# A segment loop reordered: the last keys summed in two banks, the second scores, sums and exponential moved forward

## The chip, the core and the metric

The kernel runs on one core of one Trainium2 chip. The metric is the device time of one execution in microseconds (us), as the median of several runs. TensorE multiplies matrices (PE in the profile, its weight loads PEld), VectorE and ScalarE work element by element (DVE, ACT), GpSimd does the same without access to the accumulation banks (POOL), and SyncE issues transfers (SP). All engines run at once, each through its own list of instructions in order, and wait for one another by semaphores.

## What is computed

```python
def _A_ref(x, mem0, Wq, Wk, Wv, Wo, seg_len):          # B=1, S=2048, Dm=512, H=32, Dh=128, M=8, seg_len=32
    ...
    mem = mem0
    for s in range(n_seg):                              # 64 segments
        xs = x[:, s * seg_len:(s + 1) * seg_len, :].copy()
        h = jnp.concatenate([mem, xs], axis=1)          # 8 memory rows and 32 rows of x
        q, k, v = (jnp.einsum('btd,dhe->bhte', h, W) for W in (Wq, Wk, Wv))
        scores = jnp.einsum('bhqe,bhke->bhqk', q, k) * scale
        scores = jnp.where(mask[None, None], scores, -1000000000.0)
        p = _softmax(scores, axis=-1)
        o = jnp.einsum('bhqk,bhke->bhqe', p, v)
        o = jnp.einsum('bhte,hed->btd', o, Wo)
        mem = o[:, :M, :].copy()
        outs.append(o[:, M:, :])
    return jnp.concatenate(outs, axis=1)
...
h = x + _A_ref(_layernorm(x, axis=-1), A_mem0, A_Wq, A_Wk, A_Wv, A_Wo, A_seg_len)
h2 = h + _B_ref(_layernorm(h, axis=-1), B_w_in, B_w_sp, B_b_sp, B_w_out)
```

(The three projections stand on one line here.) Block A is recurrent: the first eight rows of a segment's output are the memory rows of the next, so the 64 segments run one after another. Block B, a gated layer over the whole sequence, follows; the change doesn't touch it.

## The kernel before

Every operation is recorded through a small planner that keeps, for each engine, its instructions in the order in which the program names them, and derives the semaphore waits from tokens: a tile is read or written, and an accumulation bank is one token ("ps", bank). So the order of the calls in the loop is the order in which each engine works, and nothing is rearranged afterwards. PE's own instructions wait for PE's only through that order.

There are eight accumulation banks of 128 x 512 numbers. In the loop, a segment's inner 32 rows (8 of memory and the first 24 of x) are the stationary operand: a 128 x 32 weight, and four such products run side by side in the four column strips of the array (c = 0 to 3). Below, four matmuls that run side by side count as one group. The 512 input features are four chunks (dc), so a sum takes four groups. The 32 heads are two halves b of 16. The last 8 rows of x of each segment don't depend on the memory, and their queries, keys and values are computed ahead for 16 segments at a time.

One segment in PE's order, before the change:

- Queries (mi = 0) and keys (mi = 1) of half 0, in banks 0 and 1, eight groups by `QK`, with `mem_out` in between, which forms the second half of this segment's memory rows from the segment before (`hTm` is its token, copied by ACT at L685). `QK_evac` copies a sum to the tile Tst on ACT (L519), and DVE transposes it in 32 x 32 blocks into QT or KT (L532). `mask_put` writes the mask to the bank, onto which the scores are added.
- Queries of half 1 in bank 6, then keys of half 1 in bank 7, four groups of 512 columns each. The keys leave by two ACT copies of 256 columns and two DVE transposes (`parts` = 2).
- `S_half`, scores of half 0 (L554, L560), in bank 0; `sm_exp`, the exponential on ACT (L568), to E_sb.
- Values: `V_half` of half 0 in bank 6 and half 1 in bank 2; the first chunk of both, then the other three of half 0. `V_evac` copies them on DVE (L615).
- `sm_sums` of half 0: matmuls with ones that sum E_sb (L575, and L496 for the four that keep their weights); on ACT the logarithm `sm_ln` (L586) and `sm_rcp` (L590), an exponential of its negative, give the reciprocal of the sum.
- Scores of half 1, exponential, the last three chunks of the values of half 1, sums, logarithm, reciprocal.
- `sm_norm` multiplies E_sb by the reciprocal, in two instructions (L594 for the inner rows, L598 for the last eight): half 0 on POOL, half 1 on DVE.
- One item of work for later segments, in bank 3 (XB): a group of queries or keys (L414, four heads, 16 matmuls of 128 x 128 tiles), of values (L433), or, from segment 48 on, of block B (L775).
- `PV_half`, probabilities times values (L623, L629), both halves in banks 0, 1, 6 and 7, with the array cut by rows; copies on ACT and DVE (L642, L644); the output product of rows computed ahead (L707); the output product `Wo`, and the first half of the next memory rows.

A matmul marked as held keeps the weights that its strip has already; the others load theirs first. A held matmul has line L496 in the profile, one with a load L495. `lastop` keeps marks (the last instruction of the queries, keys, scores and values) for which transfers into reused memory wait. In segment 0 the loop also computes values ahead (`start_v`), through banks 3, 4 and 5 in turn.

Of the kernel before, what the change touches and what calls it, by code (L numbers as in the profile page):

```python
# [8 lines left out]
U32 = mybir.dt.uint32  # L9
# [160 lines left out]
def fast_path(nc, st, keep, A_x, A_mem0, A_Wq, A_Wk, A_Wv, A_Wo, A_seg_len, B_w_in, B_w_sp, B_b_sp, B_w_out, out):  # L170
# [95 lines left out]
    def PB(b):  # L266
        return ("ps", b)
# [116 lines left out]
    def slot(s):  # L384
        return s % NSLOT
# [93 lines left out]


    QKB = {(0, 0): 0, (0, 1): 1, (1, 0): 6, (1, 1): 7}
    SBK = (0, 1)
    PVB = (0, 1, 6, 7)
    VB = (6, 2)
# [16 lines left out]
    def QK(s, b, mi, dcs, first, last, held=None):  # L501
        ws = (w_q, w_k)[mi]
        bank = QKB[(b, mi)]
        sl = slot(s)
        for dc in dcs:
            for c in range(4):
                rhs = ws[:, dc, :].rearrange("p (h c i) -> p c h i", c=4, i=32)[:, c, 16 * b:16 * b + 16, :]
                pe(lambda e, dc=dc, c=c, rhs=rhs: tile_mm(e, ps[32 * c:32 * c + 32, bank, :], hT[:, sl, dc, :], rhs,
                                                          dc == first, dc == last, c, dc == held),
                   reads=[("hTx", (s // 4) % 3), ("hTm", s, dc // 2), ("W", mi, 2 * b), ("W", mi, 2 * b + 1)], writes=[PB(bank)])  # L510

    def QK_evac(s, b, mi, parts=1):
        bank = QKB[(b, mi)]
        tb = mi
        n = 8 // parts
        for k in range(parts):
            tok = [("T", tb, 0), ("T", tb, 1)] if parts == 1 else [("T", tb, k)]
            cs = slice(64 * n * k, 64 * n * (k + 1))
            act(lambda e, cs=cs: e.activation(out=Tst[:, tb, cs].rearrange("p (hp i r) -> p hp i r", i=32, r=2),  # L519
                                              in_=ps[:, bank, cs].rearrange("p (hp r i) -> p hp i r", r=2, i=32), func=ACT.Copy),  # L520
                reads=[PB(bank)], writes=tok)
        for k in range(parts):
            tok = [("T", tb, 0), ("T", tb, 1)] if parts == 1 else [("T", tb, k)]
            src = Tst[:, tb, 64 * n * k:64 * n * (k + 1)].bitcast(U32)
            hs = slice(n * k, n * (k + 1))
            if mi == 0:
                dst = QT[:, b, hs, :, :].rearrange("p hp q r -> p (hp q r)").bitcast(U32).rearrange("p (hp q) -> p hp q", hp=n)[:, :, 8:40]
                wr = [("QT", b)]
            else:
                dst = KT[:, b, hs, :, :].rearrange("p hp q r -> p (hp q r)").bitcast(U32)  # L530
                wr = [("KT", b, 0), ("KT", b, 1)] if parts == 1 else [("KT", b, k)]
            dve(lambda e, dst=dst, src=src: e.transpose(out=dst, in_=src), reads=tok, writes=wr)  # L532
# [67 lines left out]
    def V_half(s, b, dcs=range(DC), held=None):  # L600
        bank = VB[b]
        sl = slot(s)
        for dc in dcs:
            for c in range(4):
                c0 = (16 * b + 4 * c) * DH
                pe(lambda e, dc=dc, c=c, c0=c0: tile_mm(e, ps[32 * c:32 * c + 32, bank, :], hT[:, sl, dc, :], w_v[:, dc, c0:c0 + 512],
                                                        dc == 0, dc == DC - 1, c, dc == held),
                   reads=[("hTx", (s // 4) % 3), ("hTm", s, dc // 2), ("W", 2, 2 * b), ("W", 2, 2 * b + 1)], writes=[PB(bank)])

    def V_evac(b, eng):  # L610
        bank = VB[b]
        if eng == "act":
            act(lambda e: e.activation(out=V_sb[:, b, :], in_=ps[:, bank, :], func=ACT.Copy), reads=[PB(bank)], writes=[("V", b)])
        else:
            dve(lambda e: e.tensor_copy(out=V_sb[:, b, :], in_=ps[:, bank, :]), reads=[PB(bank)], writes=[("V", b)])  # L615
# [329 lines left out]
    for s in range(NSEG):  # L945
# [12 lines left out]
        if s == 4:  # L958
            load_xe(3, 1)

        QK(s, 0, 0, (0, 1), 0, 3)
        if s > 0:
            mem_out(s - 1, 1)
        QK(s, 0, 1, (1, 0), 1, 2, None if s else 1)
        QK(s, 0, 0, (2, 3), 0, 3)
        QK_evac(s, 0, 0)
        mask_put(0)
        QK(s, 0, 1, (3, 2), 1, 2, 3)
        QK_evac(s, 0, 1)
        mask_put(1)  # L970
        for mi in range(2):
            QK(s, 1, mi, ((2, 0, 1, 3), (3, 0, 1, 2))[mi], (2, 3)[mi], (3, 2)[mi], (2, 3)[mi])
            lastop["qk"[mi]] = em.by_eng["pe"][-1]
            QK_evac(s, 1, mi, 1 + mi)
        if s == 0:
            ebank[:] = [3, 4, 5]
            for n in range(2):
                start_v(n)
        S_half(s, 0)
        sm_exp(0)  # L980
        V_half(s, 0, (0,))
        if s > 0:
            V_half(s, 1, (0,), 0)
        V_half(s, 0, (1, 2, 3))
        V_evac(0, "dve")
        sm_sums(0)
        sm_ln(0)
        S_half(s, 1)
        lastop["s"] = sops[s] = em.by_eng["pe"][-1]
        sm_exp(1)  # L990
        sm_rcp(0)
        if s == 0:
            for n in range(2, 4):
                start_v(n)
        V_half(s, 1, (1, 2, 3) if s > 0 else range(DC))
        lastop["v"] = em.by_eng["pe"][-1]
        sm_sums(1)
        sm_ln(1)
        sm_rcp(1)
        if s == NSEG - 1:  # L1000
# [1107 lines left out]
```

## Time and profile before

| | |
|---|---|
| median of three runs | 855.01 us (853.56 to 855.67) |
| the profiled execution | 853.86 us |
| its span, first to last instruction | 851.7 us |
| mean granted TensorE clock | 1.000 |
| HBM traffic | 42.38 MB read, 21.59 MB written |

The profile is one execution. Its page gives busy time by engine, a chain of work followed back from the end, and groups of instructions by line; further views give the instructions in order of time. Several rows for one line are possible, since a row merges neighbours of one form. Starts and lengths are in us. Ends of matmuls are modelled: a matmul's row lasts longer than the slot after which the next begins, so PE's pace is read from starts.

### The profile page before, as it was taken

What the parts mean: (1) busy time and instruction counts of PE and PEld (TensorE: products, weight loads), DVE (VectorE), ACT (ScalarE), POOL (GpSimd) and SP (SyncE); (2) the same over time, 40 slices, a digit from 0 to 9 for tenths busy, and PEclk for the clock granted to TensorE, in tenths of its full rate; (3) what the DMA queues carried; (4) which work ended last, traced back from release to release, by engine and by line L of the source; (5) the groups of instructions that cost most, each with busy time, mean ns of one, the idle gap of its engine ahead of it and who ended that gap; (6) DMA issues with size and microseconds to landing.
All of it is one profiled execution on the core that took longest, in us unless ns stands there. A gap on an engine that the chain in (4) does not pass through costs nothing.

```text
span 851.7 us, 43893 instructions
## 1 busy us (share of the span) xinstructions
PE 837.0 (98%) x20921; PEld 447.0 (52%) x19133; DVE 538.8 (63%) x1256; ACT 427.1 (50%) x1151; POOL 159.8 (19%) x404
## 2 busy tenths in 40 slices
PE   6999999999999999999999999999999999999997
PEld 5754445555555555556555555555554544444443
DVE  3456677676666666676766666767666676553443
ACT  2455565656555655555655555565656566500000
POOL 5111121122121112121212121211112123200000
PEclk9999999999999999999999999999999999999999
DMA  9972322223212122121323222233322369032001
GB/s 319 379 227 59 75 56 57 54 47 82 57 34 75 34 65 62 26 72 47 64 58 85 55 74 51 81 70 85 91 57 80 96 184 366 2 112 105 33 12 40
DMA packets 105614, 77.21 MB, mean 91 GB/s; under 512 B 63304, under 2 KB 90960, under 8 KB 105424
## 3 DMA queue, kind: packets, MB, share of 16 engines
q1 hardware_dynamic: 105424, 74.35, 30.3%
q8 instruction: 159, 2.61, 1.3%
q14 instruction: 31, 0.25, 0.1%
HBM read 42.38 MB, written 21.59 MB: 75 GB/s over the span
## 4 chain that ended last, share of the span: by engine, by line
PE 95%; DMA 2%; SPq 1%; issue 0%; ACT 0%; DVE 0%; POOL 0%; POOLq 0%
PE f_ps L495 46%; PE f_ps L1183 11%; PE f_ps L496 8%; PE f_ps L414 6%; PE f_ps L707 4%; PE f_ps L1300 3%; PE f_ps L623 3%; PE f_ps L1176 2%; PE f_ps L433 2%; PE f_ps L775 2%; PE f_ps L554 1%; PE f_ps L575 1%; DMA f_arena<-in_A_Wk_dram 1%; PE f_ps L629 1%; PE f_ps L439 1%; PE f_ps L680 1%
## 5 line engine op out<-in xcount | busy, mean ns | idle before, releaser
L495 PE MATMUL f_ps<-f_arena,f_hT 128*32 128x512 bf16 x5120 | 359.5, 380 | 0.3
L495 PEld LDWEIGHTS f_ps<-f_arena,f_hT 128*32 128x32 bf16 x5120 | 117.0, 95 | 153.7 <-issue 63.0
L519 ACT ACTIVATE f_Tst<-f_ps 128x512 bf16<-128x512 f32 (+1 forms) x320 | 150.0, 510 | 77.5 <-PE f_ps L495 77.4
L495 PE MATMUL f_ps<-f_arena,f_cT 128*32 128x256 bf16 x3844 | 127.9, 272 | 0.7 <-ACT f_cT L642 0.5
L495 PEld LDWEIGHTS f_ps<-f_arena,f_cT 128*32 128x32 bf16 x3844 | 94.8, 96 | 27.3 <-ACT f_cT L642 18.2
L615 DVE CAST f_V_sb<-f_ps 128x512 bf16<-128x512 f32 x128 | 88.6, 692 | 25.4 <-PE f_ps L495 25.4
L1183 PE MATMUL f_ps<-f_arena 128*128 128x512 bf16 x448 | 100.9, 379 | 0.6 <-DMA f_arena<-wT_d 0.6
L532 DVE STREAM_TRANSPOSE f_QT<-f_Tst 128x256 uint32<-128x256 uint32 x128 | 57.0, 446 | 68.6 <-ACT f_Tst L519 68.5
L496 PE MATMUL f_ps<-f_arena,f_hT 128*32 128x512 bf16 x1024 | 99.8, 379 | 0.0
L539 POOL COPY f_QT<-f_arena 128x256 bf16<-128x256 bf16 x64 | 30.8, 482 | 313.3 <-PE f_ps L560 313.2
L642 ACT ACTIVATE f_cT<-f_ps 128x320 bf16<-128x320 f32 x128 | 49.0, 435 | 49.1 <-PE f_ps L629 49.1
L644 DVE TENSOR_SCALAR f_cT<-f_ps 128x320 bf16<-128x320 f32 x128 | 56.9, 487 | 25.4 <-PE f_ps L629 25.4
L532 DVE STREAM_TRANSPOSE f_KT<-f_Tst 128x128 uint32<-128x128 uint32 (+1 forms) x192 | 64.5, 349 | 12.9 <-ACT f_Tst L519 12.9
L1183 PEld LDWEIGHTS f_ps<-f_arena 128*128 128x128 bf16 x448 | 43.7, 98 | 53.4 <-DVE f_mv L723 1.0
L673 DVE CAST f_part<-f_ps 128x256 bf16<-128x256 f32 x64 | 27.2, 425 | 67.9 <-PE f_ps L495 67.9
L414 PE MATMUL f_ps<-f_hTe,f_arena 128*128 128x128 bf16 x1024 | 66.9, 223 | 2.2 <-DMA f_arena<-in_A_Wq_dram 1.4
L414 PEld LDWEIGHTS f_ps<-f_hTe,f_arena 128*128 128x128 bf16 x1024 | 59.1, 100 | 7.5 <-ACT f_hTe L395 1.6
L586 ACT ACTIVATE f_R_sb<-f_ps 128x160 f32<-128x160 f32 x128 | 39.1, 305 | 35.9 <-PE f_ps L496 32.7
L1189 DVE TENSOR_TENSOR f_arena<-f_ps,f_arena 128x512 f32<-128x512 f32 x28 | 19.3, 690 | 52.9 <-PE f_ps L1183 52.9
L685 ACT ACTIVATE f_hT<-f_ps 128x16 bf16<-128x16 f32 x126 | 23.3, 185 | 53.4 <-PE f_ps L680 53.0
L671 ACT ACTIVATE f_part<-f_ps 128x256 bf16<-128x256 f32 x64 | 24.6, 385 | 48.4 <-PE f_ps L495 48.4
L544 DVE CAST f_ps<-f_mask 128x224 f32<-128x224 bf16 x128 | 47.1, 368 | 0.0
(118 smaller groups left out, 1094.1 us busy)
## 6 DMA issues: line engine op xcount, KB each, us to landing
wT_d<-f_wst SPq DMA_DIRECT2D x32, 256.0 KB, 2.5
f_arena<-wT_d SPq DMA_DIRECT2D x32, 256.0 KB, 4.8
f_arena<-in_A_Wq_dram SPq DMA_DIRECT2D x4, 1024.0 KB, 8.7
f_arena<-in_A_Wk_dram SPq DMA_DIRECT2D x4, 1024.0 KB, 14.3
f_arena<-in_A_Wv_dram SPq DMA_DIRECT2D x4, 1024.0 KB, 14.5
f_arena<-in_A_Wo_dram SPq DMA_DIRECT2D x8, 512.0 KB, 9.5
f_Vx<-vext_d SPq DMA_DIRECT2D x63, 64.0 KB, 2.9
vext_d<-f_Vs SPq DMA_DIRECT2D x24, 128.0 KB, 2.0
```

The costliest lines, as they stand in the source:

```text
L414: pe(lambda e, h=h, dc=dc, hh=hh: e.matmul(ps[:, bank, hh * 128:(hh + 1) * 128], lhsT=ws[:, dc, h * DH:(h + 1) * DH], rhs=hTe[:, ck % 3, d ...
L495: return e.matmul(out, lhsT=lhsT, rhs=rhs, start=start, stop=stop, skip_group_check=True, tile_position=(0, 32 * c))
L496: return e.add_instruction(mybir.InstMatmult(name=nc.get_next_instruction_name(), ins=[e.lower_ap(rhs), e.lower_ap(lhsT)], outs=[e.lower_a ...
L519: act(lambda e, cs=cs: e.activation(out=Tst[:, tb, cs].rearrange("p (hp i r) -> p hp i r", i=32, r=2), in_=ps[:, bank, cs].rearrange("p (h ...
L532: dve(lambda e, dst=dst, src=src: e.transpose(out=dst, in_=src), reads=tok, writes=wr)
L544: dve(lambda e: e.tensor_copy(out=ps[:, bank, 0:224], in_=mask[:, :]), reads=["mask"], writes=[PB(bank)])
L586: act(lambda e: e.activation(out=R_sb[:, b, :], in_=ps[:, bank, 224:384], func=ACT.Ln, scale=LNS), reads=[PB(bank)], writes=[("R", b)])
L615: dve(lambda e: e.tensor_copy(out=V_sb[:, b, :], in_=ps[:, bank, :]), reads=[PB(bank)], writes=[("V", b)])
L642: act(lambda e: e.activation(out=dst, in_=src, func=ACT.Copy, scale=UNSC), reads=[PB(PVB[c])], writes=[("cT", c)])
L644: dve(lambda e: e.tensor_scalar(out=dst, in0=src, scalar1=UNSC, scalar2=None, op0=ALU.mult), reads=[PB(PVB[c])], writes=[("cT", c)])
L707: pe(lambda e, h=h, g=g, i=8 * qr + bg: e.matmul(ps[32 * g:32 * g + 32, WXB, :], lhsT=cTx[:, rb % 2, i, :], rhs=w_o[:, h, :], start=(i < 4 ...
L1183: pe(lambda e: e.matmul(ps[:, bank, 0:TB], lhsT=z2[:, sc, fb * 128:(fb + 1) * 128], rhs=wTb[tb % 2][:, :, sc, :], start=(n == 0), stop=(n ...
```

## The change

The keys of half 1 are no longer one sum over 512 columns in bank 7 but two sums over 256 columns, k = 0 in bank 3 and k = 1 in bank 7. Their groups are interleaved so that the first is complete two groups (of 256 columns) ahead of the end; each half has its own ACT copy and DVE transpose. The queries and keys of half 0 run in another order around `mem_out`, with more held weights. From segment 1 on, the sums of half 0 and the scores of half 1 come ahead of the last chunk of half 0's values, and the sums of half 1 ahead of the last chunk of half 1's. On ACT the second exponential comes ahead of the first logarithm. In segment 0 the values stay whole, and the logarithm moves too.

```diff
+    KB = (3, 7)
...
+    def K1(s, k, dc, first, last, held):
+        bank = KB[k]
+        sl = slot(s)
+        for c in range(4):
+            rhs = w_k[:, dc, :].rearrange("p (h c i) -> p c h i", c=4, i=32)[:, c, 16 + 8 * k:24 + 8 * k, :]
+            pe(lambda e, c=c, rhs=rhs: tile_mm(e, ps[32 * c:32 * c + 32, bank, 0:256], hT[:, sl, dc, :], rhs, first, last, c, held),
+               reads=[("hTx", (s // 4) % 3), ("hTm", s, dc // 2), ("W", 1, 2), ("W", 1, 3)], writes=[PB(bank)])
+
+    def K1_copy(k):
+        act(lambda e: e.activation(out=Tst[:, 1, 256 * k:256 * k + 256].rearrange("p (hp i r) -> p hp i r", i=32, r=2),
+                                   in_=ps[:, KB[k], 0:256].rearrange("p (hp r i) -> p hp i r", r=2, i=32), func=ACT.Copy),
+            reads=[PB(KB[k])], writes=[("T", 1, k)])
+
+    def K1_transpose(k):
+        src = Tst[:, 1, 256 * k:256 * k + 256].bitcast(U32)
+        dst = KT[:, 1, 4 * k:4 * k + 4, :, :].rearrange("p hp q r -> p (hp q r)").bitcast(U32)
+        dve(lambda e: e.transpose(out=dst, in_=src), reads=[("T", 1, k)], writes=[("KT", 1, k)])
...
-        QK(s, 0, 0, (0, 1), 0, 3)
+        QK(s, 0, 0, (0,), 0, 3)
+        QK(s, 0, 1, (0,), 0, 2, 0)
         if s > 0:
             mem_out(s - 1, 1)
-        QK(s, 0, 1, (1, 0), 1, 2, None if s else 1)
-        QK(s, 0, 0, (2, 3), 0, 3)
+        QK(s, 0, 1, (1,), 0, 2)
+        QK(s, 0, 0, (1, 2, 3), 0, 3, 1)
         QK_evac(s, 0, 0)
         mask_put(0)
-        QK(s, 0, 1, (3, 2), 1, 2, 3)
+        QK(s, 0, 1, (3, 2), 0, 2, 3)
         QK_evac(s, 0, 1)
         mask_put(1)
-        for mi in range(2):
-            QK(s, 1, mi, ((2, 0, 1, 3), (3, 0, 1, 2))[mi], (2, 3)[mi], (3, 2)[mi], (2, 3)[mi])
-            lastop["qk"[mi]] = em.by_eng["pe"][-1]
-            QK_evac(s, 1, mi, 1 + mi)
+        QK(s, 1, 0, (2, 0, 1, 3), 2, 3, 2)
+        lastop["q"] = em.by_eng["pe"][-1]
+        QK_evac(s, 1, 0)
+        K1(s, 0, 3, True, False, True)
+        K1(s, 1, 3, True, False, True)
+        K1(s, 0, 0, False, False, False)
+        K1(s, 1, 0, False, False, True)
+        K1(s, 0, 1, False, False, False)
+        K1(s, 0, 2, False, True, False)
+        K1_copy(0)
+        K1(s, 1, 2, False, False, True)
+        K1(s, 1, 1, False, True, False)
+        lastop["k"] = em.by_eng["pe"][-1]
+        K1_copy(1)
+        for k in range(2):
+            K1_transpose(k)
...
         S_half(s, 0)
         sm_exp(0)
-        V_half(s, 0, (0,))
-        if s > 0:
+        if s == 0:
+            V_half(s, 0)
+            V_evac(0, "dve")
+            sm_sums(0)
+            S_half(s, 1)
+        else:
+            V_half(s, 0, (0,))
             V_half(s, 1, (0,), 0)
-        V_half(s, 0, (1, 2, 3))
-        V_evac(0, "dve")
-        sm_sums(0)
-        sm_ln(0)
-        S_half(s, 1)
+            V_half(s, 0, (1, 2))
+            sm_sums(0)
+            S_half(s, 1)
+            V_half(s, 0, (3,))
+            V_evac(0, "dve")
         lastop["s"] = sops[s] = em.by_eng["pe"][-1]
         sm_exp(1)
+        sm_ln(0)
         sm_rcp(0)
...
-        V_half(s, 1, (1, 2, 3) if s > 0 else range(DC))
+            V_half(s, 1)
+            sm_sums(1)
+        else:
+            V_half(s, 1, (1, 2))
+            sm_sums(1)
+            V_half(s, 1, (3,))
         lastop["v"] = em.by_eng["pe"][-1]
-        sm_sums(1)
         sm_ln(1)
         sm_rcp(1)
```

## The prediction

> **What bounds the kernel now.** I read the page's totals first, then the chain that ended last, then one segment of the loop in order of time, and last the same place in two other kinds of segment. From the page, busy time by engine and the chain by engine:
>
> ```profile
> PE 837.0 (98%) x20921; PEld 447.0 (52%) x19133; DVE 538.8 (63%) x1256; ACT 427.1 (50%) x1151; POOL 159.8 (19%) x404
> ...
> PE 95%; DMA 2%; SPq 1%; issue 0%; ACT 0%; DVE 0%; POOL 0%; POOLq 0%
> ...
> L495 PE MATMUL f_ps<-f_arena,f_cT 128*32 128x256 bf16 x3844 | 127.9, 272 | 0.7 <-ACT f_cT L642 0.5
> ```
>
> The matmul engine is the bound nearly everywhere, so a change gains only what PE loses in short waits, and the question is which of them move. The third row says that a matmul of 256 columns lasts 0.27. The waits by pair, and one piece of the chain in order of time (start, length, what):
>
> ```profile
> PEld f_ps L575 <- ACT f_E_sb L568: 41.7, 126, 0.4
> ```
> ```profile
> 386.69 0.87 PE f_ps L495 x32
> ```
>
> Both softmax sums of all 63 later segments wait, in the record, for an exponential: 126 = 2 x 63. The chain piece gives a price: 32 matmuls of 256 columns, each with its weight load, in 0.87, so 0.109 for four that run side by side. One segment (columns: start, length, engine, line, operation, tiles, shapes, count):
>
> ```profile
> 381.17 0.39 PE L496 MATMUL f_ps<-f_arena,f_hT 128*32 128x512 bf16 x4
> ...
> 381.38 0.82 PE L495 MATMUL f_ps<-f_arena,f_hT 128*32 128x512 bf16 x12
> ...
> 382.03 0.27 PE L554 MATMUL f_ps<-f_QT,f_KT 128*32 128x40 bf16 x16
> ...
> 382.25 0.66 ACT L519 ACTIVATE f_Tst<-f_ps 128x256 bf16<-128x256 f32 x2 [0.27 <-PE f_ps L495]
> ...
> 382.67 0.59 DVE L532 STREAM_TRANSPOSE f_KT<-f_Tst 128x128 uint32<-128x128 uint32 x2 [0.20 <-ACT f_Tst L519]
> 382.80 0.36 ACT L568 ACTIVATE f_E_sb<-f_ps 128x224 bf16<-128x224 f32 x1
> 383.21 0.10 PEld L575 LDWEIGHTS f_ps<-f_E_sb,f_ones 128*32 128x32 bf16 x4 [0.30 <-ACT f_E_sb L568]
> 383.24 0.24 PE L575 MATMUL f_ps<-f_E_sb,f_ones 128*32 128x160 bf16 x4
> ...
> 383.31 0.18 PEld L554 LDWEIGHTS f_ps<-f_QT,f_KT 128*32 128x32 bf16 x16
> 383.34 0.27 PE L554 MATMUL f_ps<-f_QT,f_KT 128*32 128x40 bf16 x16
> ...
> 383.44 0.20 PE L560 MATMUL f_ps<-f_QT,f_arena 128*32 128x64 bf16 x4
> ...
> 383.47 0.82 PE L495 MATMUL f_ps<-f_arena,f_hT 128*32 128x512 bf16 x12
> 383.55 0.30 ACT L586 ACTIVATE f_R_sb<-f_ps 128x160 f32<-128x160 f32 x1 [0.39 <-PE f_ps L496]
> 383.75 0.35 ACT L568 ACTIVATE f_E_sb<-f_ps 128x224 bf16<-128x224 f32 x1
> ...
> 384.00 0.33 ACT L590 ACTIVATE f_R_sb<-f_R_sb 128x160 f32<-128x160 f32 x1
> ...
> 384.15 0.25 PE L575 MATMUL f_ps<-f_E_sb,f_ones 128*32 128x160 bf16 x4
> ...
> 384.34 0.69 DVE L615 CAST f_V_sb<-f_ps 128x512 bf16<-128x512 f32 x1 [0.18 <-PE f_ps L495]
> ...
> 384.37 1.07 PE L414 MATMUL f_ps<-f_hTe,f_arena 128*128 128x128 bf16 x16
> 384.47 0.49 POOL L594 TENSOR_TENSOR f_E_sb<-f_R_sb,f_E_sb 128x160 bf16<-128x160 f32 x1 [0.22 <-ACT f_R_sb L590]
> 384.48 0.30 ACT L586 ACTIVATE f_R_sb<-f_ps 128x160 f32<-128x160 f32 x1
> 384.81 0.34 ACT L590 ACTIVATE f_R_sb<-f_R_sb 128x160 f32<-128x160 f32 x1
> 385.04 0.30 POOL L598 TENSOR_TENSOR f_E_sb<-f_R_sb,f_E_sb 128x64 bf16<-128x64 f32 x1
> 385.18 0.34 DVE L594 TENSOR_TENSOR f_E_sb<-f_R_sb,f_E_sb 128x160 bf16<-128x160 f32 x1
> ...
> 385.37 0.27 PE L623 MATMUL f_ps<-f_E_sb,f_V_sb 32*128 32x40 bf16 x16
> 385.45 0.21 DVE L598 TENSOR_TENSOR f_E_sb<-f_R_sb,f_E_sb 128x64 bf16<-128x64 f32 x1
> ...
> 385.50 0.21 PE L629 MATMUL f_ps<-f_E_sb,f_Vx 32*128 32x64 bf16 x4
> ...
> 385.58 0.27 PE L623 MATMUL f_ps<-f_E_sb,f_V_sb 32*128 32x40 bf16 x16
> ...
> 385.72 0.21 PE L629 MATMUL f_ps<-f_E_sb,f_Vx 32*128 32x64 bf16 x4
> ...
> 385.86 0.62 PE L707 MATMUL f_ps<-f_arena,f_cTx 128*32 128x512 bf16 x8
> ```
>
> Four matmuls of 512 columns, a group from here on, take 0.216: three groups start at 381.38 and the scores follow at 382.03. Read the PE rows against that. The first sums (383.24) and second scores (383.34) follow without a gap, though their loads were released by the exponential (382.80 + 0.36 + 0.05 = 383.21) and the key transposes (382.67 + 0.59 + 0.05 = 383.31): they just fit. The second sums should start at 383.47 + 3 x 0.216 = 384.12 and start at 384.15, held by the second exponential (383.75 + 0.35 + 0.05), which itself stood behind the first logarithm on ACT. With rounding that is 0.03 to 0.04; I take 0.04. The second half of the probability-times-value matmuls (L623, 385.58) waits for DVE's normalization (385.18 + 0.34 + 0.06), and its last four (L629, 385.72) for DVE's second multiply (385.45 + 0.21 + 0.06). Other gaps (some 0.11 ahead of L414, L623 and L707) stand where the shape of the array's tiles changes; the change adds none.
>
> How long the two L623 starts lie apart tells the other kinds of segment:
>
> ```profile
> 91.34 0.27 PE L623 MATMUL f_ps<-f_E_sb,f_V_sb 32*128 32x40 bf16 x16
> ...
> 91.50 0.28 PE L623 MATMUL f_ps<-f_E_sb,f_V_sb 32*128 32x40 bf16 x16
> ```
> ```profile
> 588.98 0.27 PE L623 MATMUL f_ps<-f_E_sb,f_V_sb 32*128 32x40 bf16 x16
> ...
> 589.24 0.27 PE L623 MATMUL f_ps<-f_E_sb,f_V_sb 32*128 32x40 bf16 x16
> ```
>
> 0.16 where nothing waits (a value item is ahead), 0.21 behind L414 above, 0.26 in the late segments, whose item belongs to the second block. By the code's lists, segments 1 to 47 work off 9 value items and 38 query/key items (L414), one each, and 48 to 63 the 16 late ones.
>
> **The change, part by part, on the segment above.** *Two banks.* Four key groups become eight of 256 columns: 8 x 0.109 = 0.87 for 4 x 0.216 = 0.86, so the first scores move from 382.03 to 382.04. One more set of four weight loads hides under these groups, as the loads of the 0.87 piece do; uncovered it would cost 0.10 (the L575 load row). The first half's sum ends with the sixth group: 381.17 + 5 x 0.109 = 381.71, plus 0.01 to the fourth matmul, plus 0.27. (The old sum ended at 381.38 + 0.82 = 382.20, and the copy began 0.05 behind it.) So the first copy starts at 382.04, and the second 0.28 behind it as now (0.66 less one of 0.38, the page's 256-column copy being the same form), at 382.32, past the second half's 381.93 + 0.28 + 0.05 = 382.26: both 0.2 early. The key transposes and the first exponential follow them on DVE and ACT and are 0.20 early: KT at 383.06, E at 382.96.
>
> *The order of sums, second scores and the last quarter.* PE's new times: V groups from 382.17, first sums after four of them at 383.03, second scores 0.10 later at 383.13, last quarter 0.13 later at 383.27, then two groups of the second half, second sums at 383.91, the last group at 384.01. The loads are released at 382.96 + 0.05 = 383.01 for the sums and 383.06 + 0.05 = 383.11 for the scores: about 0.02 to spare at both, as before, so neither waits.
>
> *Second exponential first.* The scores end at 383.24 + 0.20 = 383.44 (the old L560 row, moved by 0.20 as its scores are). What ACT needs behind them when it is free the segment doesn't show: the nearest rows are 0.05 (ACT behind the key sums) and, the slowest release here, 0.14 (POOL at 384.47 behind ACT's 384.33). I take 0.06, since this is ACT behind PE: 383.50 to 383.85, and the sums' load at 383.90, against 383.91. The 0.04 goes. With 0.14 the sums wait 0.07 (B below).
>
> PE then reaches L414 at 384.01 + 0.216 + 0.105 = 384.33 (was 384.37), and L623 1.00 later at 385.33. Now the normalizations. ACT: logarithm 0.25 behind the exponential's start (383.75), reciprocal 0.33 behind that at 384.08, done 384.41, 0.08 later than now; POOL with it, its second multiply done at 385.42 for 385.34. The second logarithm follows at about 384.31 (reciprocal less the 0.10 that ACT's rows overlap, as 383.75 + 0.35 and 384.00 do), reciprocal 384.64 to 384.98, 0.17 early. DVE's value copy starts behind the last V group, 384.45 for 384.34, and ends at 385.14. DVE's multiplies come next: 385.06 if they start 0.08 ahead of the copy's end as 385.45 does ahead of 385.52, 385.14 if not, for 385.18 now. I take 385.06.
>
> So L629 of the first half needs PE's 385.46 and POOL's 385.42 + 0.06 = 385.48 (0.06 is what DVE's release takes; POOL's own is not shown): 385.48. The second L623 stands 0.03 behind it at 385.51, past DVE's 385.46, and its L629 0.12 later at 385.63, where DVE's second multiply (385.33 + 0.21 + 0.06 = 385.60) is in time. That was 385.72: **0.09 a segment**. In the late segments 0.10 of the 0.26 is a wait for DVE, so DVE, 0.12 early, could give 0.10 there, and POOL, 0.08 late, takes some back: I take 0.09 too, with 0.04 as low end. Where nothing waited there, only the 0.04 ahead of it is gained. DVE's copy of the first values, 383.71 to 384.40, is done before the second begins. Bank 3 itself is read last at the end of the segment before, twelve groups (2.6) ahead of its first key group; if that cover were gone, everything on PE would wait.
>
> Ahead of L414 there now stands a 512-column group, where short sums stood. The trace has that pair in segment 0 (the last keys, then L439 of another tile shape; the copies of those keys on ACT):
>
> ```profile
> 37.91 1.90 PE L439 MATMUL f_ps<-f_arena,f_hTe 128*128 128x512 bf16 x8
> 38.03 0.66 ACT L519 ACTIVATE f_Tst<-f_ps 128x256 bf16<-128x256 f32 x2 [0.27 <-PE f_ps L495]
> ```
>
> As 382.25 lies 0.22 behind the keys' last slot, these end theirs at 37.81, and L439 starts 0.10 later, while the last key matmuls, 0.16 longer than their slot, still run. So the gap is 0.10 to 0.11 behind either, and I keep 0.105. The Trainium skill speaks against the change here: "TensorEngine Tiling (Array Packing)", section Key Properties, has a change of tiling mode drain the engine. By a full drain L414 would start at 384.40 and 38 segments would lose 0.07 each, 2.7 of the sum.
>
> *The first queries and keys* of a segment are reordered around the memory rows: two groups ahead of them and two behind, as before; two sets of loads fewer, which lay under groups of 0.216. Nothing gained, nothing lost: the next load that waits for ACT's memory copy stands at the same place. *DMA and SP:* no transfer is issued or removed; those tied to the segment's "s" mark may start 0.2 later, and what they bring is used segments later. POOL's copy of the next memory queries waits for the second scores and is 0.2 early.
>
> *Segment 0* pays: bank 3 is the next bank of the value groups there, so L439 (37.91) must wait for the first half's copy: 0.20 ahead of 38.03, 0.38 long, 0.05 release gives 38.26: 0.35 once.
>
> **The sum:** 38 x 0.09 + 16 x 0.09 + 9 x 0.04 - 0.35 = 3.42 + 1.44 + 0.36 - 0.35 = 4.87. The profiled execution took 853.86, 851.7 of it span, so 849.0 with a span of 846.8; it lies 1.15 under the median of 855.01, so the median should be 850.1.
>
> **The rivals.** *A, the gain stops at DVE or POOL.* If the multiplies start only at 385.14, the second L623 starts at 385.54, its L629 at 385.41 + 0.21 + 0.06 = 385.68, and 0.04 is left: 54 x 0.04 + 0.36 - 0.35 = 2.2, so 852.8. The same holds if POOL's release takes 0.11 instead of 0.06. For it: a PSUM copy followed at once by these multiplies occurs nowhere in the segment. Against it: 385.45. The Trainium skill ("VectorE: DVE Perf Modes", The DRAIN you can't avoid) has the next operation wait until the pipe is empty; the 385.45 row, started before 385.52, does not bear that out. *B, the second exponential is late* by the upper bound's 0.08. Then L414 starts at 384.40, the first reciprocal ends at 384.49, POOL at 385.50, and L629 of the second half at 385.71: 54 x 0.01 - 9 x 0.03 - 0.35 = -0.1, so 855.1. For it: the fit of 0.01; against it: no ACT row here starts so late behind PE. *C, slower: the first half's copy is not released before the whole sum ends.* Place: bank 3 to ACT. Then copies start at 382.26, the first sums at 383.25 instead of 383.03, and L414 at 384.55: L629 0.13 late in 54 segments (POOL behind ACT sets it), 0.18 in nine: 7.0 + 1.6 + 0.35 = 9.0, 864.0. It decides from the point where more than 0.11 of the copies' 0.20 is lost. Against it: the first logarithm starts at 383.55, 0.05 to 0.10 behind the sums, while PE fills other banks (383.47).
>
> **How the numbers follow.** Forecast 0.60, with its own range 848.6 to 852.0; A 0.20, B 0.10, C and kin (several gates late) 0.10. No change means within 0.3%, 2.6, about what a measurement here can tell: 852.4 to 857.6. Faster: the forecast and a fifth of A, 0.64; same: the rest of A and B, 0.26; slower 0.10. The range 848.2 to 854.4 takes in A and leaves out B, C and a little of the forecast's far end.
>
> **What would show it.** In the changed profile: two copies of keys of which the first starts level with the first scores and not 0.22 behind; second sums following PE without a gap; the two L623 starts 0.18 apart; each segment 0.09 shorter there. Wrong would be a PE gap ahead of the first sums or second scores, L629 of the first half held by POOL beyond 0.03, or L414 more than 0.34 behind the last V group.

## The result and the profile after

| | before | after |
|---|---|---|
| median of the runs compared | 854.52 us (14 runs) | 857.82 us (14 runs) |
| lowest and highest | 851.92 to 857.1 | 855.78 to 859.31 |
| the profiled execution, its span | 853.86, 851.7 | 858.58, 856.4 |

The ratio after to before is 1.0036, with a 95% interval of 1.0026 to 1.0046. The change makes the kernel slower by 0.36%, some 3 us, where 4.9 us of gain were forecast. The two profiled executions lie further apart (their spans by 4.7 us) than the medians (3.3 us).

From the page of the changed kernel, busy time by engine and the chain that ended last:

```profile
PE 837.8 (98%) x21945; PEld 446.7 (52%) x18881; DVE 538.4 (63%) x1256; ACT 426.5 (50%) x1151; POOL 166.3 (19%) x404
...
PE 92%; DMA 2%; ACT 1%; SPq 1%; POOL 1%; issue 1%; DVE 0%; POOLq 0%
```

PE is as busy as before, but POOL, which got no new work, is busy for 6.5 us more (166.3 for 159.8) and now stands in the chain. The same kind of segment as in the prediction, in order of time (start, length, engine, line, operation, tiles, shapes, count, and the idle time before it with what ended it):

```profile
384.08 0.39 PE L497 MATMUL f_ps<-f_arena,f_hT 128*32 128x256 bf16 x8
...
384.95 0.27 PE L573 MATMUL f_ps<-f_QT,f_KT 128*32 128x40 bf16 x16
384.96 0.66 ACT L522 ACTIVATE f_Tst<-f_ps 128x256 bf16<-128x256 f32 x2
...
385.37 0.59 DVE L529 STREAM_TRANSPOSE f_KT<-f_Tst 128x128 uint32<-128x128 uint32 x2
...
385.94 0.24 PE L594 MATMUL f_ps<-f_E_sb,f_ones 128*32 128x160 bf16 x4
...
386.04 0.27 PE L573 MATMUL f_ps<-f_QT,f_KT 128*32 128x40 bf16 x16
...
386.15 0.20 PE L579 MATMUL f_ps<-f_QT,f_arena 128*32 128x64 bf16 x4
...
386.42 0.36 ACT L587 ACTIVATE f_E_sb<-f_ps 128x224 bf16<-128x224 f32 x1 [0.56 <-PE f_ps L579]
...
386.62 1.46 DVE L634 CAST f_V_sb<-f_ps 128x512 bf16<-128x512 f32 x2 [0.66 <-PE f_ps L496]
...
386.83 0.25 PE L594 MATMUL f_ps<-f_E_sb,f_ones 128*32 128x160 bf16 x4
...
386.94 0.39 PE L496 MATMUL f_ps<-f_arena,f_hT 128*32 128x512 bf16 x4
...
387.26 1.07 PE L414 MATMUL f_ps<-f_hTe,f_arena 128*128 128x128 bf16 x16
387.49 0.49 POOL L613 TENSOR_TENSOR f_E_sb<-f_R_sb,f_E_sb 128x160 bf16<-128x160 f32 x1 [0.56 <-ACT f_R_sb L609]
...
387.99 0.32 DVE L613 TENSOR_TENSOR f_E_sb<-f_R_sb,f_E_sb 128x160 bf16<-128x160 f32 x1
388.06 0.42 POOL L617 TENSOR_TENSOR f_E_sb<-f_R_sb,f_E_sb 128x64 bf16<-128x64 f32 x1
388.23 0.33 DVE L617 TENSOR_TENSOR f_E_sb<-f_R_sb,f_E_sb 128x64 bf16<-128x64 f32 x1
...
388.26 0.27 PE L642 MATMUL f_ps<-f_E_sb,f_V_sb 32*128 32x40 bf16 x16
388.52 0.10 PEld L648 LDWEIGHTS f_ps<-f_E_sb,f_Vx 32*128 32x128 bf16 x4
388.53 0.21 PE L648 MATMUL f_ps<-f_E_sb,f_Vx 32*128 32x64 bf16 x4
...
388.57 0.26 PE L642 MATMUL f_ps<-f_E_sb,f_V_sb 32*128 32x40 bf16 x16
...
388.67 0.19 PE L648 MATMUL f_ps<-f_E_sb,f_Vx 32*128 32x64 bf16 x4
```

The last keys start at 384.08 here and at 381.17 in the prediction's segment, so 2.91 added to a time of the prediction gives the place to look for it. Everything down to the L642 row at 388.26 stands within 0.03 of its forecast. Then the pattern breaks: the last four matmuls of the first half (L648) stand at 388.53 and not at 388.39. Their weights could be loaded 0.04 after POOL's second multiply, 388.06 + 0.42 = 388.48. That multiply lasted 0.30 before. Now two multiplies of DVE run at the same time, and the second of these takes 0.33 where it took 0.21. The groups by line between 130 and 690 us (busy us, mean ns of one, idle time before) show that this is so in all segments, first before, then after:

```profile
L598 POOL TENSOR_TENSOR f_E_sb<-f_R_sb,f_E_sb 128x64 bf16<-128x64 f32 x56 | 17.3, 309 | 4.4
...
L598 DVE TENSOR_TENSOR f_E_sb<-f_R_sb,f_E_sb 128x64 bf16<-128x64 f32 x55 | 11.7, 213 | 0.0
```
```profile
L617 POOL TENSOR_TENSOR f_E_sb<-f_R_sb,f_E_sb 128x64 bf16<-128x64 f32 x55 | 22.8, 414 | 4.3
...
L617 DVE TENSOR_TENSOR f_E_sb<-f_R_sb,f_E_sb 128x64 bf16<-128x64 f32 x55 | 18.1, 330 | 0.0
L613 DVE TENSOR_TENSOR f_E_sb<-f_R_sb,f_E_sb 128x160 bf16<-128x160 f32 x55 | 17.5, 318 | 0.0
```

POOL's multiply of 64 columns takes 105 ns more and DVE's 117 ns more. The Trainium skill has a rule for this, on the page "SBUF — State Buffer", section Who interferes with whom: DVE's second read interface is the one that GpSimd reads through, and whoever has it locks the other out. The trace agrees on who waits: DVE's first multiply, which was already running, isn't stretched (318 ns), POOL's starts inside it and is stretched, and DVE's second is stretched in turn. It doesn't show how long each is locked out: POOL's multiply lies beside DVE's first for 0.25 us (from 388.06 to 387.99 + 0.32) and is only 0.11 longer. No run separates this rule from another cost of working at the same time.

How long a segment takes is read from one first-scores row to the next. For example after, before (where the first row is the prediction's 382.03), and in the first experiment below:

```profile
384.95 0.27 PE L573 MATMUL f_ps<-f_QT,f_KT 128*32 128x40 bf16 x16
...
395.09 0.27 PE L573 MATMUL f_ps<-f_QT,f_KT 128*32 128x40 bf16 x16
```
```profile
392.15 0.27 PE L554 MATMUL f_ps<-f_QT,f_KT 128*32 128x40 bf16 x16
```
```profile
382.39 0.27 PE L573 MATMUL f_ps<-f_QT,f_KT 128*32 128x40 bf16 x16
...
392.43 0.27 PE L573 MATMUL f_ps<-f_QT,f_KT 128*32 128x40 bf16 x16
```

That is 10.14, 10.12 and 10.04. The table gives such lengths in us for segments 1 to 62, as the median of each kind: 9 with a value item, 30 with a query or key item until 450 us, and 23 later ones (one fewer of the second and one more of the third where a kernel is slower). Its last column sums what single segments lie above (or a little below) their kind's median; the larger of these are stops of PE, treated further below. Each kernel was profiled once.

| kernel | value item | query or key item | later | sum above the medians |
|---|---|---|---|---|
| before | 10.080 | 10.120 | 10.095 | 2.6 |
| after | 10.128 | 10.146 | 10.124 | 4.2 |
| logarithm first | 10.087 | 10.042 | 10.015 | 4.6 |
| exponential first, alone | 10.285 | 10.307 | 10.286 | 3.8 |
| DVE behind POOL | 10.340 | 10.399 | 10.369 | 1.8 |
| split alone | 10.091 | 10.126 | 10.100 | 2.8 |
| logarithm first, no split | 10.280 | 10.234 | 10.204 | 4.4 |

Of the 4.7 us between the two spans, the segments' lengths give 9 x 0.048 + 30 x 0.026 + 23 x 0.029 = 1.9, and the last column gives 1.6. Another 0.4 lies in segment 0, where the forecast had 0.35 for L439's wait for the first key copy; its row, at 37.91 before, after the change is:

```profile
38.28 1.04 PE L439 MATMUL f_ps<-f_arena,f_hTe 128*128 128x512 bf16 x4 [0.27 <-ACT f_Tst L522]
```

And 0.4 lies at the first matmul of block B's main product, which waits for weights; the last 0.4 was not placed. From the groups by line, before and after:

```profile
L1183 PE MATMUL f_ps<-f_arena 128*128 128x512 bf16 x448 | 100.9, 379 | 0.6 <-DMA f_arena<-wT_d 0.6
```
```profile
L1225 PE MATMUL f_ps<-f_arena 128*128 128x512 bf16 x448 | 100.9, 379 | 1.0 <-DMA f_arena<-wT_d 1.0
```

### The profile page after: what moved, and what is told of

It is laid out like the page before. It is cut to its first block, busy times and chain, and to the rows that moved or that the text cites. A ratio compares the mean times of both kernels' runs of the same rounds, so it can differ in the third digit from the quotient of the medians.

```text
span 856.4 us, 44663 instructions
## 1 busy us (share of the span) xinstructions
PE 837.8 (98%) x21945; PEld 446.7 (52%) x18881; DVE 538.4 (63%) x1256; ACT 426.5 (50%) x1151; POOL 166.3 (19%) x404
## 4 chain that ended last, share of the span: by engine, by line
PE 92%; DMA 2%; ACT 1%; SPq 1%; POOL 1%; issue 1%; DVE 0%; POOLq 0%
PE f_ps L496 40%; PE f_ps L497 12%; PE f_ps L1225 11%; PE f_ps L414 6%; PE f_ps L726 4%; PE f_ps L1342 3%; PE f_ps L1218 2%; PE f_ps L433 2%; PE f_ps L642 2%; PE f_ps L648 2%; PE f_ps L573 1%; DMA f_arena<-in_A_Wk_dram 1%; PE f_ps L594 1%; PE f_ps L794 1%; PE f_ps L439 1%; PE f_ps L699 1%
## 5 line engine op out<-in xcount | busy, mean ns | idle before, releaser
L496 PE MATMUL f_ps<-f_arena,f_hT 128*32 128x512 bf16 (+1 forms) x4868 | 356.9, 357 | 1.1 <-issue 0.9
L496 PEld LDWEIGHTS f_ps<-f_arena,f_hT 128*32 128x32 bf16 x4868 | 122.1, 95 | 155.9 <-issue 69.3
L497 PE MATMUL f_ps<-f_arena,f_hT 128*32 128x512 bf16 x2300 | 183.9, 331 | 0.0
L538 ACT ACTIVATE f_Tst<-f_ps 128x512 bf16<-128x512 f32 x192 | 107.7, 595 | 61.7 <-PE f_ps L496 61.7
L414 PE MATMUL f_ps<-f_hTe,f_arena 128*128 128x128 bf16 x1024 | 66.5, 222 | 2.9 <-DMA f_arena<-in_A_Wq_dram 2.1
L414 PEld LDWEIGHTS f_ps<-f_hTe,f_arena 128*128 128x128 bf16 x1024 | 58.8, 99 | 12.9 <-issue 11.4
L587 ACT ACTIVATE f_E_sb<-f_ps 128x224 bf16<-128x224 f32 x128 | 46.1, 360 | 36.5 <-PE f_ps L579 36.5
L683 POOL COPY f_cTx<-f_cT 128x256 bf16<-128x256 bf16 x64 | 25.5, 398 | 102.0 <-DVE f_cT L663 102.0
```

What stands on the lines that cost most here:

```text
L414: pe(lambda e, h=h, dc=dc, hh=hh: e.matmul(ps[:, bank, hh * 128:(hh + 1) * 128], lhsT=ws[:, dc, h * DH:(h + 1) * DH], rhs=hTe[:, ck % 3, d ...
L496: return e.matmul(out, lhsT=lhsT, rhs=rhs, start=start, stop=stop, skip_group_check=True, tile_position=(0, 32 * c))
L497: return e.add_instruction(mybir.InstMatmult(name=nc.get_next_instruction_name(), ins=[e.lower_ap(rhs), e.lower_ap(lhsT)], outs=[e.lower_a ...
L587: act(lambda e: e.activation(out=E_sb[:, b, :], in_=ps[:, bank, 0:224], func=ACT.Exp, scale=scale, bias=SHIFT), reads=[PB(bank)], writes=[ ...
```

## The experiments

P is the theory that the new order on ACT makes POOL late while DVE comes early, so that the two multiply at the same time, slow each other and hold PE. Q is the rival that the loss lies in another part of the change. Times of before beside each group of runs differ a little, since each group was measured on one chip with its own runs of before: 853.93 us (23 runs) for the first four, 854.41 (27) for the next four, 854.06 (23) for the last four.

### The logarithm first again, all else as changed

```diff
-        sm_exp(1)
         sm_ln(0)
+        sm_exp(1)
         sm_rcp(0)
```

> The changed kernel with one line moved back: on ACT the first logarithm ahead of the second exponential again. Theory P (POOL's multiplies start late behind the reciprocal, and their second one collides with DVE's): POOL starts about 0.3 us earlier in each segment, its second multiply is back near 310 ns from 414, the last four matmuls of the first probability-times-value half (L648) wait for nothing, the second sums wait 0.04 again; a segment with a key item takes about 10.06 instead of 10.146, the kernel 851 to 852.5. Rival Q (the sum in two banks, or the supply of its 770 more instructions, costs the time): no change, 857 to 858.5.

Measured: 853.48 us (12 runs), ratio to before 0.9997, interval 0.9988 to 1.0007. The whole loss is gone. The groups between 130 and 690 us, and the end of the segment whose last keys start at 381.51:

```profile
L617 POOL TENSOR_TENSOR f_E_sb<-f_R_sb,f_E_sb 128x64 bf16<-128x64 f32 x56 | 17.4, 311 | 4.4
L617 DVE TENSOR_TENSOR f_E_sb<-f_R_sb,f_E_sb 128x64 bf16<-128x64 f32 x56 | 12.4, 221 | 0.0
```
```profile
381.51 0.39 PE L497 MATMUL f_ps<-f_arena,f_hT 128*32 128x256 bf16 x8
...
384.30 0.25 PE L594 MATMUL f_ps<-f_E_sb,f_ones 128*32 128x160 bf16 x4
...
385.18 0.31 POOL L617 TENSOR_TENSOR f_E_sb<-f_R_sb,f_E_sb 128x64 bf16<-128x64 f32 x1
385.46 0.32 DVE L613 TENSOR_TENSOR f_E_sb<-f_R_sb,f_E_sb 128x160 bf16<-128x160 f32 x1
...
385.99 0.21 PE L648 MATMUL f_ps<-f_E_sb,f_Vx 32*128 32x64 bf16 x4
```

Counted from the last keys, POOL's second multiply starts at 3.67 (3.98 after the change) and is all but over (385.18 + 0.31 = 385.49) when DVE begins, at 3.95 (3.91). The second sums start at 2.79 for 2.75: that 0.04 is all that the exponential's place had won on PE, and it cost POOL 0.31. The last L648 starts at 4.48, for 4.59 after and 4.55 before. So P stands. But P had expected 851 to 852.5; the missing part is taken up below.

### The new order on ACT alone, in the kernel before

```diff
         sm_sums(0)
-        sm_ln(0)
         S_half(s, 1)
...
         sm_exp(1)
+        sm_ln(0)
         sm_rcp(0)
```

> The kernel of before with only the order on ACT changed: second exponential ahead of the first logarithm. Theory P: POOL's first multiply starts about 0.27 us later than before, and its second collides with DVE's: L629 of the first half waits, 0.2 us a segment, so 864 to 868 with the collision, about 860 if the multiplies keep their 309 and 213 ns. Rival Q: the second sums lose their wait of 0.04 and nothing else moves, 852 to 855.

Measured: 865.37 us (4 runs), ratio 1.0136, interval 1.0118 to 1.0153: P, with the collision's price in it. Nothing else stands earlier here, so POOL's multiplies start the whole 0.31 later than before (median of the 38 segments with a query or key item, counted from the first scores), where in the changed kernel it is 0.10. Groups between 130 and 690 us:

```profile
L598 POOL TENSOR_TENSOR f_E_sb<-f_R_sb,f_E_sb 128x64 bf16<-128x64 f32 x54 | 20.1, 372 | 4.2
L629 PE MATMUL f_ps<-f_E_sb,f_Vx 32*128 32x64 bf16 x432 | 18.2, 191 | 8.9 <-POOL f_E_sb L598 8.6
...
L598 DVE TENSOR_TENSOR f_E_sb<-f_R_sb,f_E_sb 128x64 bf16<-128x64 f32 x54 | 17.8, 330 | 0.0
```

The two multiplies stretch here too (372 and 330 ns), with none of the other parts in the kernel, and PE's wait is now put down to POOL by name.

### The changed kernel, with DVE's multiplies held until POOL's are done

```diff
         sm_norm(0, pool)
         V_evac(1, "dve")
-        sm_norm(1, dve)
+        pool_done = em.by_eng["pool"][-1]
+        sm_norm(1, lambda fn, **k: dve(fn, after=[pool_done], **k))
```

> The changed kernel with DVE's two multiplies held until both of POOL's are done, a wait more. Theory P: without an overlap POOL's second multiply takes 300 to 315 ns (now 414) and DVE's second 205 to 220 (now 330), the first L648 starts 0.1 earlier relative to its segment, but the second half waits for DVE, so the kernel is 10 to 16 us slower than the changed one. If there is no collision, both durations stay at 414 and 330.

Measured: 871.65 us (one run). Keeping the two apart by a wait costs more than the collision, as expected; the run was made for the lengths:

```profile
L617 POOL TENSOR_TENSOR f_E_sb<-f_R_sb,f_E_sb 128x64 bf16<-128x64 f32 x54 | 16.5, 306 | 4.2
L617 DVE TENSOR_TENSOR f_E_sb<-f_R_sb,f_E_sb 128x64 bf16<-128x64 f32 x54 | 11.8, 218 | 0.0
```

ACT's order and the instructions are those of the changed kernel; only the overlap is gone, and 414 and 330 ns are 306 and 218 again. So the stretch comes from the overlap. What it costs PE shows in the first half's last two rows of a segment:

```profile
394.18 0.27 PE L642 MATMUL f_ps<-f_E_sb,f_V_sb 32*128 32x40 bf16 x16
394.33 0.21 PE L648 MATMUL f_ps<-f_E_sb,f_Vx 32*128 32x64 bf16 x4
```

L648 stands 0.15 behind L642, which is the prediction's 385.48 - 385.33; in the changed kernel it stands 0.27 behind (388.53 - 388.26). POOL's lateness alone would have cost PE no more than was forecast; the other 0.12 is the collision's.

### The split of the last keys alone, in the kernel before

The edit puts the eight `K1` calls, their copies and transposes in place of the old key sum; nothing else moves.

> The kernel of before with only the second half's keys summed in two banks. Theory P: 0.01 us a segment for the eight shorter groups and 0.35 once in segment 0, so about 1 us over before: 855 to 856. Rival Q: 3 us or more over before, 857.5 or more.

Measured: 854.7 us (12 runs), ratio 1.0005, interval 0.9993 to 1.0017. The time lies 0.3 under P's range, but 0.8 over before, near the 1 us that P had. The segments are 5 to 11 ns longer, the forecast's 0.01. So P again: the loss isn't the split's.

### The logarithm first, without the split

```diff
-        K1(s, 0, 3, True, False, True)
...
-        for k in range(2):
-            K1_transpose(k)
+        QK(s, 1, 1, (3, 0, 1, 2), 3, 2, 3)
+        lastop["k"] = em.by_eng["pe"][-1]
+        QK_evac(s, 1, 1, 2)
```

> The changed kernel with the first logarithm ahead of the second exponential and the last K summed in one bank as before; second scores and sums stand where the change puts them. Theory P (the split is what makes the early second scores possible: without it the second half of the transposed K comes 0.2 us later, and the second scores, which now start right behind their gate, wait 0.1 to 0.15 us in each of 63 segments): time 856 to 861. Rival (the transposes are early enough anyway, the split only adds instructions): 851.5 to 853.5.

Measured: 863.3 us (5 runs), ratio 1.01, interval 1.0086 to 1.0115: 0.19 us a segment more than with the split, so the split is needed, and for more than P's 0.1 to 0.15: the time lies 2.3 above P's range. PE waits at another place first, too. In order of time:

```profile
387.76 0.66 ACT L538 ACTIVATE f_Tst<-f_ps 128x256 bf16<-128x256 f32 x2 [0.27 <-PE f_ps L496]
...
388.10 0.60 PE L496 MATMUL f_ps<-f_arena,f_hT 128*32 128x512 bf16 x8
388.18 0.59 DVE L551 STREAM_TRANSPOSE f_KT<-f_Tst 128x128 uint32<-128x128 uint32 x2 [0.20 <-ACT f_Tst L538]
388.30 0.36 ACT L587 ACTIVATE f_E_sb<-f_ps 128x224 bf16<-128x224 f32 x1
...
388.72 0.25 PE L594 MATMUL f_ps<-f_E_sb,f_ones 128*32 128x160 bf16 x4
...
388.83 0.27 PE L573 MATMUL f_ps<-f_QT,f_KT 128*32 128x40 bf16 x16
```

The first sums could start at 388.10 + 2 x 0.216 = 388.53, and wait until 388.72 for the first exponential, which stands behind the two key copies on ACT. That is the 0.19. The transposed keys alone would have held the second scores about as long: 388.18 + 0.59 + 0.05 = 388.82, and the scores start at 388.83. So the split makes both the exponential and the transposed keys early enough; by these rows, either one late would cost about 0.19.

### Where the rest of the gain went: stops of PE

With the logarithm first, the segments are shorter than before by 30 x 0.078 + 23 x 0.080 - 9 x 0.007 = 4.1 us, but the times show only 0.5. Of its profile, 4.6 - 2.6 = 2.0 us went into the last column of the table, and 1.1 into the first matmul of block B's product (1.7 of idle time for 0.6). The larger entries of that column are single stops of PE that no semaphore ends. Before, and after:

```profile
337.10 0.39 PE L433 MATMUL f_ps<-f_arena,f_hTe 128*32 128x512 bf16 x3
337.81 0.38 PE L433 MATMUL f_ps<-f_arena,f_hTe 128*32 128x512 bf16 x1 [0.33 <-issue]
```
```profile
237.76 0.39 PE L496 MATMUL f_ps<-f_arena,f_hT 128*32 128x512 bf16 x2
238.87 0.39 PE L496 MATMUL f_ps<-f_arena,f_hT 128*32 128x512 bf16 x2 [0.71 <-issue]
```

Both fall in the middle of four matmuls that run side by side. In the fourteen profiles there are 45 such stops over 0.3 us between 85 and 690 us. By the records of the transfers, 44 of them end 2.2 to 3.2 us after the start of a 16 KB packet of the instruction queue (one, with the exponential first alone, 3.5). These packets start 4.3 to 4.5 us apart on average; the one ahead of a stop starts 4.5 to 7.0 us behind its predecessor, so it is late. Two theories were tried: that transfers which transpose block B's weights make these packets late (T), and that it depends on where the packets' ends fall in the stream (V).

```diff
-        sp(lambda e: e.dma_start_transpose(out=wst[:, :, :], in_=B_w_sp[i * 64:(i + 1) * 64, :]), writes=["wst"])
+        sp(lambda e: e.dma_start(wst[:].rearrange("p a b -> p (a b)"),
+                                 B_w_sp[i * 64:(i + 1) * 64, :].rearrange("r (h x) -> (r h) x", h=2)), writes=["wst"])
```

In the kernel before:

> The kernel before, with the second stage's weights loaded by a plain transfer of the same bytes in place of the transposing transfer (the weights then stand in another order, so the output differs; the work of every engine is the same). In the traces so far TensorE stops now and then for 0.3 to 0.9 us at single places (337.8, 427.0 in before; 177.5, 238.9, 318.0, 564.6 in after; 237.1, 315.9, 428.2, 560.8 in the run with the logarithm first), each time 5 to 8 us after a transposing transfer was issued, and no semaphore ends the stop. Theory T (the block of instructions that TensorE needs comes late because the transposing transfer holds the DMA engines): the stops over 0.3 us in the segments are gone, and the time falls by 1 to 2 us, to 852 to 853.5. Rival U (the stops belong to the instruction stream, and the transfers have nothing to do with them): the stops stay, time 853.5 to 854.5.

In the changed kernel:

> The changed kernel with the same plain transfer (output in another order). Theory T: stops over 0.3 us gone, time 854.5 to 856.5 for 857.8, and the difference to before with the plain transfer is what the segments show, 26 ns x 30 + 48 ns x 9 + 29 ns x 23 = 1.9 us. Rival U: stops stay, time 857 to 858.5, difference to before with the plain transfer 3 to 4 us.

In the one with the logarithm first:

> The changed kernel with the first logarithm ahead of the second exponential, with the same plain transfer (output in another order). Its key-item segments are 78 ns and its late ones 80 ns shorter than those of before in the traces, its value-item ones 7 ns longer: 30 x 78 + 23 x 80 - 9 x 7 = 4.1 us, of which the times showed 0.5. Theory T: the stops took the rest: time 849 to 851, 2.5 to 4.5 us under before with the plain transfer. Rival U: 853 to 854, and 0 to 1 us under before with the plain transfer.

Measured, 11 runs each: 853.37 us (ratio 0.9995, interval 0.9984 to 1.0006), 856.23 (1.0027, 1.0014 to 1.0039) and 852.52 (0.9978, 0.9968 to 0.9988). The sums of the table's last column stay at 2.6, 4.2 and 4.3 us, with stops over 0.3 us still there (at 439.2, 177.9 and 236.9 us, for example). T, which had none left, falls by that. The times alone wouldn't decide: the first two lie in T's ranges, the third between T's and U's. The medians lie 1.0 to 1.6 us under those with the transposing transfer, but for the kernel before the interval takes in no change, and for the other two the counterparts were measured in other groups of runs; this was not followed up. The order of the three kernels is the same as with the transposing transfers, which is a second measurement of it: +2.9 for the changed kernel, -0.9 with the logarithm first.

Then 64 or 32 tiny matmuls were put at the start, ahead of the first weights:

```diff
     xT(0, 6)
+    for _ in range(64):
+        pe(lambda e: e.matmul(ps[0:32, 1, 0:8], lhsT=ident[:, 0:32], rhs=ident[:, 0:8], start=True, stop=True,
+                              skip_group_check=True, tile_position=(0, 0)), reads=["ident"], writes=[PB(1)])
     xe_copy(0, 6)
```

Before, with 64:

> The kernel before with 64 tiny matmuls (8 columns, into a bank that nothing reads then) at the start, while TensorE waits for the first weights: every later TensorE instruction stands 128 instructions further on in the instruction stream, half of one of the 16 KB packets in which the instruction queue brings it, if one instruction takes 64 bytes (162 packets for 44663 instructions say 276 each). The plain transfer took no stop away, so the stops are looked for in the stream. Theory V (a stop comes where the end of a packet falls on a stretch of short matmuls): the sum of the stops changes by 1 us or more, either way, and the time with it (852 to 853 or 855 to 857). Rival W (the stops don't depend on it): sum of stops 2.6 us as in both profiles of this stream, time 853.5 to 855.

The changed kernel, with 64:

> The changed kernel with the same 64 tiny matmuls at the start. Theory V: the sum of its stops, 4.2 us in both profiles of this stream, changes by 1 us or more; if it falls to the 2.6 of before, the time is 855.5 to 856.5. Rival W: 857 to 858.5. In both the segments keep their lengths: 10.146 (key items), 10.126 (value items), 10.124 (late).

The logarithm first, with 64, and with 32:

> The changed kernel with the first logarithm ahead of the second exponential, with the same 64 tiny matmuls. Theory V: sum of stops other than 4.3 to 4.6 us by 1 us or more; with 2.6 us the time is 851 to 852, the 0.35% under before that the segments promise. Rival W: 853 to 854.

> The same with 32 tiny matmuls, a quarter of a packet. Theory V: another sum of stops than without and with 64, time 850.5 to 856. Rival W: 853 to 854, as without them.

Measured: 855.03 us (11 runs; 1.0006, interval 0.9996 to 1.0016), 856.93 (7 runs; 1.0032, 1.0021 to 1.0043), 851.65 (5 runs; 0.9965, 0.9952 to 0.9979) and 853.61 (11 runs; 0.9989, 0.9979 to 0.9999). The segments keep their lengths to 4 ns. The sums of the last column are 3.9, 2.0 and 3.4 us with 64, where they were 2.6, 4.2 and 4.6, and 4.4 with 32. Each is from one profile, so how far such a sum varies between runs of one kernel isn't shown.

The places say more. Five profiles have the changed kernel's list of instructions on PE (the changed kernel, the logarithm first, both with the plain transfer, and DVE behind POOL). Of their 19 stops, 15 fall on five places, the same matmul of the same segment (in one case the matmul next to it), each of which two to four of the five profiles share. The changed kernel's stop at 238.87 is that of 237.13 with the logarithm first; those at 564.63 and 560.77 are another such pair. In the three profiles with the list of before, 6 of 10 stops fall on three shared places. With 64 matmuls ahead, the changed kernel and the logarithm first share two places, 4 of their 6 stops, and none of the five old places has a stop any more.

So a stop hangs on where an instruction stands in PE's list, and 128 more instructions at the start move the stops. Here V holds. That the end of a packet is what counts isn't shown. For the times V is borne out once only. Before and the changed kernel moved the way their sums did, up and down, but within the intervals; the changed kernel missed V's range. The logarithm first with 64 left its old interval (0.9965 for 0.9997 of before), and its profile shows 1.1 us less in the last column. That profile is of its slowest run (854.51 us; the other four took 851.0 to 852.1), which waits 2.7 us at the first matmul of block B's product. With 32 the sum changed by 0.2 only, and the time lies in W's range. Why a packet comes late at some places and not at others, and what makes that last wait vary from nothing to 2.7 us between the profiles, stays open.

The version with the logarithm first and 64 matmuls has the lowest time against before, with 5 runs behind it: 0.35% less, by its interval 0.21% to 0.48%.

## Why the prediction was wrong, point by point

- **Two banks:** right. First scores at 384.95 (forecast 382.04 + 2.91), first copy level with them at 384.96, transposed keys at 385.96 (385.97). The split alone costs 0.01 a segment, and without it the rest doesn't pay.
- **Sums and second scores ahead of the last quarter:** right to 0.01 (385.94, 386.04), with no gap of PE.
- **The second exponential behind the scores:** right. It starts 0.07 after them (386.42 against 386.15 + 0.20), where 0.06 was taken; the second sums stand at 386.83 for 386.82. Rival B, a late second exponential, didn't come, nor did C: the first copy started before the second half's sum was complete.
- **L414 behind a long group:** right. It starts 387.26 - 386.94 - 0.216 = 0.10 after the last group's slot. The rule of a drain (the Trainium skill, "TensorEngine Tiling (Array Packing)", Key Properties), as the prediction worked it out, was to put L414 at 384.40 + 2.91 = 387.31, and that is not borne out in this pair either. The gap of 0.10 is there all the same; since ends of matmuls are modelled, the rows don't show whether the array is empty in it.
- **DVE's multiplies ahead of the copy's end:** right. They start at 387.99, and the copies end at 386.62 + 1.46 = 388.08; so rival A's first form didn't come.
- **POOL 0.08 late:** right in its cause, and 0.11 when measured (387.49 - 384.08 = 3.41 for 3.30); POOL's release takes 0.04, not more than the 0.06 taken.
- **"its second multiply done at 385.42 for 385.34": this is the step that failed.** It took POOL's multiply at the 0.30 of the trace before, although the same paragraph moved DVE's multiplies from 385.18 to 385.06, into POOL's time. With 0.42 it was done at 385.57 of that clock, L629 of the first half stood 0.14 late, the second L623 0.15 and the last L629 0.13. So 0.09 of gain a segment became 0.04 of loss in this stretch, 0.026 over the whole segment. Of POOL's 0.15, 0.03 is the later start and 0.12 the longer multiply. The sign that the prediction gave came, L629 held by POOL beyond 0.03: PE could have begun it at 388.26 + 0.13 = 388.39, and the two L623 starts lie 0.31 apart, not 0.18. It is the place that rival A named ("if POOL's release takes 0.11"), by another mechanism and at more than twice its price: A allowed for 0.05, the collision took 0.11. Slower had a chance of 0.10, given to C and its kin, whose mechanism is not this one.
- **Where nothing waited before** (value items), 0.04 of gain was forecast and 0.048 of loss measured; in the late segments 0.09 of gain and 0.029 of loss. Both lie 0.09 to 0.12 off, by the same step.
- **Segment 0:** right, 0.37 for 0.35.
- **What the forecast had no term for:** the last column of the table, stops for the larger part, rose by 1.6 of the 4.7 us between the two profiles. With the logarithm first the segments gain 4.1 us, near the 5.2 that the forecast had for them, and the median still moves by 0.5 only (853.48 for a forecast of 850.1). So a kernel in which POOL's step had held would probably have missed the forecast time as well.

The trace of before did hold a sign, though a weak one. DVE's multiply of 160 columns took 342 ns there, starting at 385.18 while POOL's second ran (385.04 + 0.30); where it starts at POOL's end, with the logarithm first, it takes 316, and 325 where it is held until POOL's is done. What two engines cost each other can be read only where a trace has the instruction both alone and beside the other.

## What to carry to other kernels

When a change brings an instruction of one engine forward and delays one of another, lay both new intervals side by side: if DVE and GpSimd then multiply SBUF operands at the same time, as here, don't count on the durations of the old trace. A swap in one engine's queue has two prices, what the first of the two wins and what everything behind the second loses; here 0.04 on PE was bought with 0.31 on POOL. And where the gain is below half a per cent, compare lengths of equal stretches, not only the total: two programs can also differ by where in their instruction lists PE stops.

## What the runs showed of the hardware that was not expected

- Multiplies of two SBUF operands on DVE and GpSimd, 128 x 64, take 414 and 330 ns (GpSimd and DVE) where they overlap in the changed kernel, 372 and 330 with the exponential first alone, 306 and 218 where they don't overlap. The one that runs already is hardly slowed (318 ns for 316 at 160 columns, in the changed kernel).
- PE stops for 0.3 to 1.3 us at single places, between matmuls of one group, with no semaphore behind it. They are the larger part of the 1.8 to 4.6 us that 62 segments take above the medians of their kinds. Kernels with the same list of instructions on PE stop largely at the same instructions; 128 instructions more at the start move the places, and the sum above the medians then differed by up to 2.2 us.
